# Full-tile V and P·V passes, remainders in either order, and a layer lag of eight in a two-layer segment-recurrent transformer kernel

## The chip, the cores and the metric

One NeuronCore of a Trainium2 chip runs the whole program. The metric is the device time of that core in microseconds (us). The kernel before takes 2775.58 us (median of 4 runs, 2775.19 to 2778.07). A ratio in this text is the mean time of one kernel's fast runs over the mean of the other's fast runs of the same rounds, so it is not quite the ratio of the medians that are quoted beside it. TensorE's matrix unit is called PE, VectorE DVE, ScalarE ACT.

## The reference

Two layers, each an attention block A with a recurrent memory and a feed-forward block B. The sequence of 2048 positions is cut into 64 segments of 32; eight memory columns come out of each segment and go into the next.

```python
for s in range(n_seg):                       # 64 segments, strictly one after the other
    h = concatenate([mem, x[segment s]])     # 8 + 32 = 40 rows of width 576
    q, k, v = h@Wq, h@Wk, h@Wv               # 32 heads of 128
    p = softmax(mask(q k^T * scale))
    o = (p v) @ Wo
    mem = o[:8]; out = o[8:]
# B: out = (silu(x@w1) * (x@w3)) @ w2        # 576 -> 4608 -> 576
x = x + A(layernorm(x)); x = x + B(layernorm(x))   # twice, with the same weights
```

## The kernel before

Layer 1 runs `LAG` segments behind layer 0, so most steps work on two segments at once (80 columns: 2 x 40). The work is cut into nodes, and a string of letters fixes PE's order: Q/q the Q/K projection and its 64-row remainder (576 = 4 x 128 + 64), S scores, T transposes of P, X/x and V/v the V projections of new x and of memory, P for P times V, O/o the output projection, F/f/W the feed-forward block. An opening string is followed by a block of four steps, repeated 11 times, and an end string. PE's results go to a memory called PSUM; there are seven banks of it (`bank` in the lines below) for everything but the output sum (`YB`).

```python
LAG = 7
...
def v_mm(self, t, b, strips, tail):          # V in strips of 32 columns, four side by side
    for c in ((4,) if tail else range(4)):
        for r in (0, 1):
            for p0, c0, q in strips:
                out = self.bk(b[r])[p0:p0 + 32, :]
                if tail: ...                 # 64-row remainder, eight strips side by side
                else:
                    w0 = ...
                    self.mm(out, HTt[:, c, c0:c0 + 32], W[:, c, w0:w0 + 512], c == 0, False, tile_position=(0, p0))
...
def pv(self, t, g, pts, vx, vm, b):          # 64-row halves: V of x and V of memory
    for hl in range(4):
        for m, s in todo:
            for ab in (0, 1):
                rr = slice(ab * R64, (ab + 1) * R64)
                self.mm(self.bk(b[ab])[...], self.T.V[rr, s.i, g % 2, ...], PT[rr, m, hl, :],
                        m == todo[0][0], m == 1, tile_position=(ab * R64, 0))
...
def load_v(self):                            # 512 rows in four loads of 128, the remainder in two of 64 partitions
    for c in range(4):
        self.dma(self.wv(False)[:, c, :], self.a.wv[c * P:(c + 1) * P, :])
    t = self.a.wv[4 * P:D, :].rearrange("p (k r n) -> p k r n", k=2, r=2)
    for r in (0, 1):
        self.dma(self.wv(True)[r * R64:(r + 1) * R64, :].rearrange("p (k n) -> p k n", k=2), t[:, :, r, :])
```

## Time and profile before

| | before |
|---|---|
| time, median | 2775.58 us |
| span of the profiled run | 2772.4 us |
| PE busy, PE idle | 2723.5 us, 48.9 us |
| DVE, ACT busy | 2047.1 us, 1091.0 us |
| PE idle in the first 100 us | 31.5 us |
| matmuls, changes of tile shape | 60919, 2138 |
| one block of four steps | 162.2 us |

Names in the profile lines, here and in the prediction: HT is the transposed input of attention; W, WV and WO are weights (W holds those of Q and K, and in turn those of the feed-forward block); QKT is Q and K, PB and PTS the probabilities before and after their transposes, XTB the transposed input of the feed-forward block. `64*128 64x80` is the part of PE's array in use (rows * columns), then the operand that streams through it (partitions x columns).

### The profile page before, as it was taken

The numbers are of one execution on the slowest core, as the hardware profiler recorded it, in microseconds if no ns is written. First come the engines' busy times: TensorE is split into PE (matmuls) and PEld (weight loads), VectorE is DVE, ScalarE is ACT, GpSimd is POOL, SyncE is SP. The second block draws the span as 40 slices with busy tenths as digits, with TensorE's granted clock in tenths as the row PEclk, the third lists the DMA queues.
The fourth block names the chain that finished last, engine by engine and source line by source line (L and its number), as shares of the span: only waits on it lengthen the run. The fifth ranks groups of instructions, "written<-read, shape, count | busy, mean of one in ns | idle before, by whom it ended". The sixth has DMA issues, their size and how long they took to land.

```text
span 2772.4 us, 136269 instructions
## 1 busy us (share of the span) xinstructions
PE 2723.5 (98%) x60919; PEld 2252.7 (81%) x60919; DVE 2047.1 (74%) x5584; ACT 1091.0 (39%) x3339; POOL 328.4 (12%) x399
## 2 busy tenths in 40 slices
PE   5999999999999999999999999999999999999999
PEld 4887888888888888888888888888888888878887
DVE  4677777777777777777777777777777777687776
ACT  1434343433434343343434334343433434343332
POOL 1111010110101011010101101010101101010110
PEclk9999999999999999999999999999999999999999
DMA  8062614244242424424152342415234241523467
GB/s 308 13 198 69 184 53 138 81 121 124 78 131 62 140 82 116 128 78 131 56 146 82 112 133 77 131 49 153 82 106 138 73 130 57 142 79 107 141 182 235
DMA packets 481691, 322.02 MB, mean 116 GB/s; under 512 B 26216, under 2 KB 476656, under 8 KB 479440
## 3 DMA queue, kind: packets, MB, share of 16 engines
q1 hardware_dynamic: 478080, 306.38, 37.7%
q8 instruction: 476, 7.80, 1.2%
q0 software_dynamic: 3024, 6.93, 0.9%
q14 instruction: 111, 0.91, 0.1%
HBM read 308.49 MB, written 2.36 MB: 112 GB/s over the span
## 4 chain that ended last, share of the span: by engine, by line
PE 96%; DMA 2%; ACT 1%; DVE 1%; issue 0%; SPq 0%; ACTq 0%; DVEq 0%
PE bank L547 82%; PE YB L547 14%; DMA W<-in_A_Wk_dram 1%; DMA W<-in_B_w_dram 1%; DMA WV<-in_B_w_dram 0%; SPq L556 0%; DMA W<-in_A_Wq_dram 0%; ACT OT L550 0%; DVE STAT L553 0%; ACT HT L550 0%; DVE SME L553 0%; ACT PTS L550 0%; DVE PB L553 0%; DVE PTS L553 0%; ACT QKT L550 0%
## 5 line engine op out<-in xcount | busy, mean ns | idle before, releaser
L547 PEld LDWEIGHTS <-W 128*128 128x128 bf16 (+1 forms) x29080 | 1231.6, 98 | 144.4 <-issue 37.7
L547 PE MATMUL bank<-HT,W 128*128 128x80 bf16 (+3 forms) x22720 | 816.4, 198 | 23.1 <-DMA W<-in_A_Wk_dram 12.1
L547 PE MATMUL bank<-XTB,W 128*128 128x256 bf16 (+1 forms) x6360 | 658.2, 261 | 1.6 <-ACT XTB L550 0.8
L906 POOL MEMSET PB<- 128x1024 bf16 x284 | 270.0, 951 | 2065.9 <-PE bank L547 1626.9
L550 ACT ACTIVATE QKT<-bank 128x64 bf16<-128x64 f32 (+1 forms) x1348 | 312.6, 315 | 445.0 <-PE bank L547 434.4
L547 PE MATMUL YB<-OT,WO 128*128 128x80 bf16 (+3 forms) x11360 | 429.2, 199 | 5.0 <-ACT OT L550 3.9
L547 PEld LDWEIGHTS <-WO 128*128 128x128 bf16 (+1 forms) x11360 | 385.2, 102 | 36.0 <-issue 17.4
L547 PE MATMUL bank<-WV,HT 128*32 128x512 bf16 (+1 forms) x6840 | 380.8, 382 | 0.0
L553 DVE CAST QKT<-bank 128x64 bf16<-128x64 f32 (+1 forms) x716 | 193.6, 316 | 243.5 <-PE bank L547 242.3
L547 PE MATMUL bank<-W2C,HTT 128*128 128x288 bf16 x2240 | 312.5, 287 | 0.2 <-issue 0.2
L553 DVE TENSOR_REDUCE STAT<-SME 104x8 f32<-104x320 f32 (+1 forms) x568 | 271.5, 478 | 44.8 <-ACT SME L550 41.2
L553 DVE TENSOR_TENSOR PB<-SME,STAT 40x128 bf16<-40x128 f32 (+1 forms) x1004 | 283.7, 321 | 12.9 <-DVE STAT L553 0.5
L547 PEld LDWEIGHTS <-HT 128*32 128x32 bf16 (+1 forms) x6840 | 150.2, 95 | 173.4 <-issue 48.1
L547 PEld LDWEIGHTS <-HTT 128*128 128x128 bf16 x2304 | 211.5, 98 | 57.4 <-issue 4.9
L553 DVE SCALAR_TENSOR_TENSOR XR<-bank,XR 128x288 f32<-128x288 f32 x576 | 241.2, 447 | 10.6 <-PE bank L547 4.6
L550 ACT ACTIVATE HTT<-bank 128x512 bf16<-128x512 f32 (+1 forms) x324 | 175.0, 549 | 182.8 <-PE bank L547 182.6
L550 ACT ACTIVATE SME<-SME 104x320 f32<-104x320 f32 (+1 forms) x284 | 133.4, 470 | 262.0 <-DVE SME L553 261.6
L553 DVE SCALAR_TENSOR_TENSOR HTT<-HTT,bank 128x512 bf16<-128x512 bf16 (+1 forms) x324 | 201.5, 622 | 41.2 <-ACT HTT L550 39.1
L550 ACT ACTIVATE PTS<-bank 128x320 bf16<-128x320 f32 (+1 forms) x386 | 146.5, 411 | 206.1 <-PE bank L547 143.0
L550 ACT ACTIVATE OT<-bank 128x320 bf16<-128x320 f32 (+1 forms) x358 | 141.1, 413 | 212.4 <-PE bank L547 212.0
L553 DVE TENSOR_TENSOR HTT<-HTT,bank 128x512 bf16<-128x512 bf16 (+1 forms) x324 | 203.6, 628 | 24.2
L550 ACT ACTIVATE V<-bank 128x512 bf16<-128x512 f32 x269 | 147.2, 596 | 173.9 <-PE bank L547 173.4
(64 smaller groups left out, 1676.3 us busy)
## 6 DMA issues: line engine op xcount, KB each, us to landing
W<-in_B_w_dram SPq DMA_DIRECT2D x612, 256.0 KB, 3.8
W2C<-in_B_w_dram SPq DMA_DIRECT2D x306, 288.0 KB, 3.2
W<-in_B_w_dram SPq DMA_DIRECT2D x612, 32.0 KB, 3.3
W<-in_B_w_dram SPq DMA_DIRECT2D x10, 512.0 KB, 8.2
WO<-in_A_Wo_dram SPq DMA_DIRECT2D x4, 1152.0 KB, 17.2
XR<-in_A_x_dram POOLq DMA_DIRECT2D x16, 288.0 KB, 3.1
W<-in_A_Wq_dram SPq DMA_DIRECT2D x4, 1024.0 KB, 8.4
W<-in_A_Wk_dram SPq DMA_DIRECT2D x4, 1024.0 KB, 15.0
```

The costliest lines, as they stand in the source:

```text
L547: self.ch("PE", self.nc.tensor.matmul(out, lhsT=lhsT, rhs=rhs, start=start, stop=stop, skip_group_check=True, **k))
L550: self.ch("ACT", self.nc.scalar.activation(*a, **k))
L553: self.ch("DVE", getattr(self.nc.vector, fn_)(*a, **k))
L906: return lambda n: self.ch("POOL", self.nc.gpsimd.memset(self.T.PB[:, pb.i], 0.0))
```

## The change

The intent is to spend less of PE on narrow tiles and on changing between tile shapes. V of the next segment's x and of this segment's memory share one full 128-column pass; P times V has one 128-row matmul per head instead of two 64-row halves; a main part and its remainder may run in either order, so that remainders can stand together; layer 1 runs eight steps behind. The weight loads change too: Q and K come in halves of the heads, and each 64-row remainder is folded onto 128 partitions in one transfer. In the new strings G and g are the full V pass and its remainder, p the transposes of the attention output, and w a second kind of W node.

```diff
-LAG = 7
+LAG = 8
...
+    def vg(self, t, g, b, tail):
+            for c in ((4,) if tail else range(4)):
+                for r in (0, 1):
+                    if tail: ...
+                    else:
+                        self.mm(self.bk(b[r])[:], HTt[:, c, 32:160], W[:, c, w0:w0 + 512], first and c == 0, c == 3)
...
-            for hl in range(4):
-                for m, s in todo:
-                    for ab in (0, 1):
-                        ... 64-row halves ...
+            for j in range(GH):
+                self.mm(self.bk(b[j // 4])[:, ...], self.T.V[:, self.head(g, j) // 4, ...],
+                        self.T.PTS[:, pts.i, j * nq:(j + 1) * nq], True, True)
...
+            for kind, wd in ((0, self.a.wq), (1, self.a.wk)):
+                self.dma(self.T.W[:, 8, kind * 2048:(kind + 1) * 2048], wd[4 * P:D, :].rearrange("p (r n) -> r p n", r=2))
...
+        return lambda n: self.dma(self.wv(True), self.a.wv[4 * P:D, :].rearrange("p (r n) -> r p n", r=2))
... (new order strings, slot bookkeeping, evictions of V by rows, W_O in eight loads, first loads of x and memory from ACT's queue)
```

## The prediction

> **What bounds the kernel now.** I read the page first: busy shares, then the chain that ended last, then PE's waits, then PE's timeline in a quiet stretch, because everything above says that only PE's own time counts.
>
> ```profile
> span 2772.4 us, 136269 instructions
> PE 2723.5 (98%) x60919; PEld 2252.7 (81%) x60919; DVE 2047.1 (74%) x5584; ACT 1091.0 (39%) x3339; POOL 328.4 (12%) x399
> PE 96%; DMA 2%; ACT 1%; DVE 1%; issue 0%; SPq 0%; ACTq 0%; DVEq 0%
> ```
>
> The reader is to see that PE is idle for 2772.4 - 2723.5 = 48.9 us in all, and that 96% of the chain is PE following PE. Where the idle time lies comes from the busy time by stretch (stretch, its length, then busy us of PE, PEld, DVE, ACT, POOL):
>
> ```profile
> 0.00:100.00 100.00, 68.47 (x1903) 53.56 (x1903) 50.91 (x142) 28.49 (x93) 17.86 (x34) 0.93 0.62 215
> 1000.00:1500.00 500.00, 499.23 (x10828) 415.20 (x10825) 374.82 (x1023) 201.87 (x611) 58.27 (x70) 1.00 0.36 105
> 1500.00:2000.00 500.00, 499.23 (x10844) 413.35 (x10838) 377.70 (x1029) 206.13 (x625) 57.51 (x68) 1.00 0.36 102
> ```
>
> The opening 100 us hold 31.5 us of the idle time, most of it the weights' arrival; in the middle it is 0.8 us in 500. So in the middle the time is the sum of what PE executes, and to price the change I need what each kind of matmul takes from its start to the start of the next. The mean duration of a row (about 200 ns) is latency and useless for this. The timeline of PE (start, length, instruction, count) gives it:
>
> ```profile
> 1418.13 4.19 PE L547 MATMUL bank<-WV,HT 128*32 128x512 bf16 x80
> 1422.25 0.43 PE L547 MATMUL bank<-QKT 128*64 128x40 bf16 x16
> ...
> 1429.79 1.15 PE L547 MATMUL bank<-W2C,HTT 128*128 128x288 bf16 x8
> 1430.77 1.31 PE L547 MATMUL bank<-HT,W 128*128 128x80 bf16 x32
> 1431.92 1.91 PE L547 MATMUL bank<-XTB,W 128*128 128x256 bf16 x16
> 1433.76 0.46 PE L547 MATMUL bank<-PTS,V 64*128 64x80 bf16 x16
> 1434.06 0.38 PE L547 MATMUL bank<-XTB,W 64*128 64x256 bf16 x4
> 1434.28 0.31 PE L547 MATMUL bank<-HT,W 64*128 64x80 bf16 x8
> 1434.52 2.47 PE L547 MATMUL YB<-OT,WO 128*128 128x80 bf16 x64
> 1436.82 0.45 PE L547 MATMUL bank<-sel,PB 104*128 104x80 bf16 x8
> 1437.20 0.34 PE L547 MATMUL YB<-OT,WO 128*64 128x80 bf16 x8
> ```
>
> Read it by differences of starts. Full tile, 80 columns: (1431.92 - 1430.77)/32 = 36 ns; the 64 of W_O: 2.30/64 = 36 ns. Full tile, 288 columns: 0.98/8 = 123 ns. P times V today is 16 matmuls of 64 rows, two side by side: 0.30 us, so 36 ns for a pair. The Q/K remainder is 4 pairs, 0.144 us, but 0.24 us pass before the next full-tile matmul: 0.096 us more. The transposes of P are 8 x 36 = 0.288 us, but 0.38 us pass before the next column-tiled one: 0.092 us more. Those two surpluses stand exactly where the tile shape changes. V: 80 rows are 16 passes of four strips and 2 of eight; 18 x 0.216 = 3.89 us (0.216 is the spacing of 512-column passes over the whole trace), and 4.12 us pass with two changes of shape: 0.23 for two. Over all 2138 changes the median surplus is close to 0.0975 us, whichever two shapes meet; I use that.
>
> Check of the rule on the kernel before: its 60919 matmuls priced so give 2507 us, its 2138 shape changes (counted in the built instruction list) 208 us, idle time 49 us; sum 2764 against a span of 2772.4. The 8 us left are 0.3%, partly the opening's granted clock of 0.93 in the stretch above.
>
> **What the Trainium skill says.** "TensorEngine Tiling (Array Packing)", Key Properties: changing the tiling mode drains the engine. It gives no figure; this trace gives 0.092 to 0.115 us. "TensorE: Matmul & The Clock Gate", "Wait — 56ns, not 53.3ns?": a warm matmul is spaced by N / 2.4 GHz plus about 2.5 ns, never under about 25 ns. For 80 columns that is 35.8 ns and for 512 it is 216 ns; the trace agrees (36 and 216). For 40 columns the floor holds: the trace's median is 25 ns, so a step with one layer costs more than half of a step with two. The same page, Part 3, "The mechanism": tiles in different row or column groups run concurrently, some 4 ns apart; the 16 in 0.30 us agree. "Perfetto Trace Analysis", "Optimization Strategy": a gap that repeats on the saturated engine can mean too few PSUM buffers. The kernel before has no such gap; the change could make one.
>
> **The change, part by part.** Counts before and after are from the two built programs.
>
> P times V in full tiles: 3712 half-row matmuls of 80 columns (1856 pairs at 36 ns) become 1792 full ones at 36 ns, and the 40-column ones likewise. A pair costs what a full one costs, so work alone does not fall (77.2 to 77.4 us). What falls is the shape: P times V no longer leaves the full shape.
>
> V in one pass: for two steps with both layers the old way was 5 nodes of 9 passes of 512 columns in strips; the new is 4 full-tile nodes and one in strips, again 45 passes. Again no work saved in the middle; at the ramps some passes go, and all V passes together fall from 332.4 to 319.1 us: -13.3.
>
> Layer 1 eight steps behind instead of seven: 56 steps of both layers and 16 of one, instead of 58 and 13. Q/K matmuls of 80 columns fall by 512 and of 40 rise by 768, and so on: Q/K projections +2.1, W_O +1.3, transposes, P times V and scores about -0.1. With the +0.2 of P times V already inside, +3.3.
>
> Remainders in either order and the new order: these let 64-row nodes stand next to each other. In the block of four steps, repeated 11 times, the changes of shape fall from 114 to 73: -41 x 0.0975 = -4.0 us of a block that lasts 162.2 us today (the same run of matmuls recurs at 1036.19, 1198.40 and 1360.61 us in the chain). In the whole program they fall from 2138 to 1430: -708 x 0.0975 = -69.0 us. All of it lies on PE, and PE is the path.
>
> Sum of PE: -13.3 + 3.3 - 69.0 = -79 us.
>
> Beside PE: V is copied out of PSUM in 342 instructions now (269 ACT, 73 DVE) and in 864 then, since each bank holds rows for different places. One of 512 columns takes 596 ns on ACT and 689 on DVE, however many partitions. At the new split (560 and 304) V adds 173 us to ACT and 159 to DVE. Q/K copies move the other way, from DVE to ACT. With the durations of the rows before I estimate DVE 2047 to about 2105 us (78% of a shorter span) and ACT 1091 to about 1355 (50%). Neither becomes the bound on average.
>
> The loads are split by head halves, so first Q/K work can start earlier, but V and W_O arrive as late as before (the first V matmul stood at 43.55 us). I give -2 us. For new waits I add 5 us. Span 2772.4 - 79 - 2 + 5 = 2696; measured times are 3.5 us over the span (2775.85 against 2772.4): 2700 us, 2.7% less.
>
> **The rivals.** First, PSUM: a full-tile V node holds two of seven banks from its first matmul until half is copied, P times V of that group has run, and the other half is copied. A wait of 0.1 us in each of 288 groups would be 29 us and the result 2724: within 2%. For it speaks that seven banks serve everything and DVE is busier; against it, that PE waits 0.8 us per 500 today with nodes held just as long between main part and remainder. Second, the drains might hide copies PE would otherwise wait for; then removing them turns them into waits, and only some 20 us come off: 2755. For it: nearly every change of shape is a new node. Against: the same surplus at any two shapes, and almost no waits beside it. Third, V and P times V themselves get faster in full tiles, by fewer weight loads; then 2670. Against: spacing already equals the streaming of columns. Fourth, the extra one-layer steps starve at the ends: the recurrence has less to hide behind; 5 to 10 us.
>
> **Range and chances.** Work and shape changes are counted, their prices measured to perhaps 8%: +-6 us. The skew is upward, from waits. Range 2672 to 2732. The 2% line is 2720.3, so 20 us of unforeseen waits are needed to miss it: faster 0.82, same 0.17, slower 0.01.
>
> **What would show it.** Right: PE still 98% busy, a block of four steps near 158 us, P times V as 8 matmuls in about 0.29 us with no surplus, full V passes of 0.216 us, PE idle about 50 us in all. Wrong: PE waiting for V or bank copies by ACT or DVE over and over in the middle (first rival), surplus still 0.1 us at each new node without a change of shape (second), or idle time in the first 100 us well over 31 us (fourth).

## More of the kernel before

The prediction shows how the middle is read. Here is what it passed over quickly, the opening. First, who PE waited for (us in total, times, longest), then the queue that issues the loads (start, time taken, what, how many):

```profile
PE bank L547 <- DMA W<-in_A_Wk_dram: 12.1, 5, 3.0
```

```profile
6.92 0.55 SPq L556 DMA_DIRECT2D W<-in_A_Wq_dram  x1
9.40 0.47 SPq L556 DMA_DIRECT2D W<-in_A_Wk_dram  x1
11.88 13.71 SPq L556 DMA_DIRECT2D WV<-in_A_Wv_dram  x6
27.40 19.65 SPq L556 DMA_DIRECT2D WO<-in_A_Wo_dram  x4
```

The reader is to see that the weights set the pace of the first 30 us, in an orderly row: the two lone transfers of W are the 64-row remainders, V follows at 11.88 us, and W_O at 27.40.

## The result, and the profile after

The changed kernel takes 2748.91 us (median of 4 runs, 2746.57 to 2753.3; ratio 0.9904, 95% interval 0.989 to 0.9918). It is correct and 1% faster, where 2.7% was forecast, and the time lies above the stated range. Against the 2% line it counts as the same, to which the prediction gave 0.17. The profiled run is the slowest of the four. Its head and its chain by engine:

```profile
span 2751.5 us, 126617 instructions
PE 2657.0 (97%) x55783; PEld 2234.0 (81%) x55783; DVE 2137.9 (78%) x5480; ACT 1362.0 (49%) x3920; POOL 333.2 (12%) x400
PE 91%; DVE 3%; ACT 2%; DMA 2%; issue 1%; SPq 1%; POOL 0%; DVEq 0%; ACTq 0%
```

PE's busy time fell by 66.5 us, but PE now idles 2751.5 - 2657.0 = 94.5 us, 45.6 more than before. The busy time by stretch (same columns as in the prediction) says where:

```profile
0.00:100.00 100.00, 40.48 (x1038) 31.51 (x1039) 37.56 (x98) 21.27 (x59) 11.29 (x24) 0.86 0.65 214
1000.00:1500.00 500.00, 497.12 (x9889) 417.82 (x9886) 400.01 (x1015) 251.46 (x730) 57.13 (x68) 1.00 0.37 106
```

The first 100 us hold 59.5 us of idle time instead of 31.5. The middle holds 2.9 in 500 instead of 0.8. Both traces keep every matmul of their programs (60919 and 55783), so the boundaries between opening, blocks and end are found by counting, and each stretch can be compared with its price: matmuls at the durations of the prediction, plus 0.0975 us for each change of shape.

| stretch (us) | before | priced for after | after | PE idle, before to after |
|---|---|---|---|---|
| opening | 549.9 | 549.9 - 11.4 - 160 x 0.0975 = 522.9 | 558.7 | 37.0 to 67.7 |
| 11 blocks | 1784.5 | 1784.5 - 451 x 0.0975 = 1740.5 | 1750.4 | 2.8 to 10.6 |
| end | 434.1 | 434.1 + 1.4 - 97 x 0.0975 = 426.0 | 438.1 | 5.2 to 12.0 |

Of the excess over the price, 35.8 + 9.9 + 12.1 = 57.8 us, the opening has 62%, and the growth of idle time explains 45.3 (30.7 of it in the opening). The other 12.5 us stand in no wait that the profile lists; a lower granted clock (0.86 against 0.93 in the first 100 us) or an error of the prices would do, and neither was tested. So the opening is the first thing to ask about. Whom PE waited for, over the whole run:

```profile
PE bank L580 <- DMA W<-in_A_Wk_dram: 19.2, 7, 12.8
PE bank L580 <- DMA WV<-in_A_Wv_dram: 13.0, 3, 9.4
...
PE bank L580 <- DVE HT L586: 8.8, 11, 0.8
PE bank L580 <- DMA W<-in_A_Wq_dram: 8.4, 1, 8.4
```

Three single waits, 12.8, 9.4 and 8.4 us, are 30.6 us. PE's timeline shows what stands behind them:

```profile
26.24 0.21 PE L580 MATMUL bank<-HT,W 64*128 64x40 bf16 x2 [8.36 <-DMA W<-in_A_Wq_dram]
39.30 0.96 PE L580 MATMUL bank<-HT,W 64*128 64x40 bf16 x30 [12.84 <-DMA W<-in_A_Wk_dram]
...
70.91 3.99 PE L580 MATMUL bank<-WV,HT 64*32 64x512 bf16 x48 [9.39 <-DMA WV<-in_A_Wv_dram]
```

All three are matmuls of 64 rows: the remainders of Q, K and V, which are the three loads that were folded into one transfer each. The queue that issues them, and the share of the 16 DMA engines in use (next to last column) in stretches before and during such a load:

```profile
6.82 0.63 SPq L589 DMA_DIRECT2D W<-in_A_Wq_dram  x1
7.55 4.66 SPq L589 DMA_DIRECT2D W<-in_A_Wk_dram  x1
12.26 18.67 SPq L589 DMA_DIRECT2D W<-in_A_Wq_dram  x4
```

```profile
8.00:12.00 4.00, 0.94 (x10) 0.66 (x10) 2.23 (x10) 0.96 (x1) 0.56 (x1) 1.00 1.03 380
16.00:20.00 4.00, 1.88 (x57) 1.76 (x53) 0.00 (x0) 0.00 (x0) 0.00 (x0) 1.00 0.13 53
```

Between 16 and 20 us the DMA engines move 53 GB/s at a share of 0.13, which is 0.13 x 16 = 2.1 engines' worth, and only packets of 4096 bytes pass. Each took 159 ns, so a load of 128 such packets on two engines takes 64 x 0.159 = 10.2 us. V's remainder agrees: PE's last V matmuls before it could start at 60.47 us, those of the remainder at 70.91, 10.4 us later. The four loads behind took 18.67 us to issue, where comparable ones in the first microseconds took 2.66.

The middle agrees with the prices. Full V and P times V in a block:

```profile
857.25 2.22 PE L580 MATMUL bank<-WV,HT 128*128 128x512 bf16 x10
859.31 1.56 PE L580 MATMUL bank<-HT,W 64*128 64x80 bf16 x40
...
872.90 0.45 PE L580 MATMUL bank<-PTS,V 128*128 128x80 bf16 x8
873.19 3.15 PE L580 MATMUL YB<-OT,WO 128*128 128x80 bf16 x96
```

Eight full V passes and a pair of remainders take 2.06 us: 9 x 0.216 + 0.0975 = 2.04. Eight P times V take 0.29 us, with no surplus before W_O. A block lasts 159.2 us (the same run of matmuls recurs at 1354.82, 1513.98 and 1673.19 us), priced at 158.2. Over the ten blocks from 717 to 2309 us, the list of PE's waits has one entry:

```profile
PE bank L580 <- DVE HT L586: 8.0, 10, 0.8
```

It is 0.8 us at each block's start. The new block opens with two 64-row remainders, which need the memory columns as DVE has summed them; the timeline there shows PE going on at 1513.79, when the first of DVE's two additions is done (it ends at 1513.73; the line gives the two together):

```profile
1513.30 0.23 ACT L583 ACTIVATE YO<-YB 64x80 f32<-64x80 f32 x1
1513.57 0.36 DVE L586 TENSOR_TENSOR HT<-YB,YO 64x16 bf16<-64x16 f32 x2 [2.02 <-ACT YO L583]
1513.79 1.90 PE L580 MATMUL bank<-HT,W 64*128 64x80 bf16 x48 [0.80 <-DVE HT L586]
```

### The profile page after: what moved, and what is told of

Its sections match the earlier page's. It is cut to its first block, busy times and chain, and to the rows that moved or that the text cites.

```text
span 2751.5 us, 126617 instructions
## 1 busy us (share of the span) xinstructions
PE 2657.0 (97%) x55783; PEld 2234.0 (81%) x55783; DVE 2137.9 (78%) x5480; ACT 1362.0 (49%) x3920; POOL 333.2 (12%) x400
## 4 chain that ended last, share of the span: by engine, by line
PE 91%; DVE 3%; ACT 2%; DMA 2%; issue 1%; SPq 1%; POOL 0%; DVEq 0%; ACTq 0%
PE bank L580 79%; PE YB L580 13%; ACT V L583 1%; DMA WV<-in_A_Wv_dram 1%; SPq L589 1%; DVE V L586 1%; DVE STAT L586 1%; DVE SME L586 1%; DMA W<-in_A_Wk_dram 1%; DVE XR L586 0%; ACT SME L583 0%; DMA W<-in_A_Wq_dram 0%; DVE PB L586 0%; DMA W<-in_B_w_dram 0%; ACT HT L583 0%
## 5 line engine op out<-in xcount | busy, mean ns | idle before, releaser
L580 PE MATMUL bank<-XTB,W 128*128 128x256 bf16 (+3 forms) x6360 | 652.3, 262 | 2.2 <-ACT XTB L583 1.4
L583 ACT ACTIVATE QKT<-bank 128x256 bf16<-128x256 f32 (+2 forms) x1533 | 373.5, 307 | 361.7 <-PE bank L580 339.3
L580 PE MATMUL YB<-OT,WO 128*128 128x80 bf16 (+3 forms) x11520 | 409.6, 198 | 5.0 <-issue 4.6
L583 ACT ACTIVATE V<-bank 32x512 bf16<-32x512 f32 (+1 forms) x560 | 318.4, 585 | 144.6 <-PE bank L580 139.3
L580 PE MATMUL bank<-WV,HT 128*32 128x512 bf16 (+4 forms) x3240 | 369.8, 385 | 13.0 <-DMA WV<-in_A_Wv_dram 13.0
L586 DVE TENSOR_TENSOR PB<-SME,STAT 40x128 bf16<-40x128 f32 (+4 forms) x912 | 275.7, 336 | 15.0 <-DVE STAT L586 0.5
L580 PEld LDWEIGHTS <-HT 128*32 128x32 bf16 (+4 forms) x3240 | 138.4, 96 | 160.9 <-issue 39.9
L583 ACT ACTIVATE OT<-bank 128x320 bf16<-128x320 f32 (+1 forms) x403 | 150.5, 404 | 183.1 <-PE bank L580 180.6
L586 DVE CAST V<-bank 64x512 bf16<-64x512 f32 (+1 forms) x304 | 208.1, 685 | 34.0 <-PE bank L580 27.9
L586 DVE CAST QKT<-bank 128x128 bf16<-128x128 f32 (+4 forms) x515 | 141.5, 316 | 105.3 <-PE bank L580 102.4
```

The lines of the kernel that those rows point to most:

```text
L580: self.ch("PE", self.nc.tensor.matmul(out, lhsT=lhsT, rhs=rhs, start=start, stop=stop, skip_group_check=True, **k))
L583: self.ch("ACT", self.nc.scalar.activation(*a, **k))
L586: self.ch("DVE", getattr(self.nc.vector, fn_)(*a, **k))
```

## The experiments

The theory, T: a folded remainder load runs on two DMA engines and holds up what is issued after it. Rivals: R, the half-row loads with their small packets and greater number are slow; S, one-layer steps starve for the recurrence, whatever the loads do. The base for runs 1 to 3 is the changed kernel. All eight runs gave correct results.

**Run 1, remainder loads cut in two.**

```diff
-                self.dma(self.T.W[:, 8, kind * 2048:(kind + 1) * 2048], wd[4 * P:D, :].rearrange("p (r n) -> r p n", r=2))
+                for r in (0, 1):
+                    self.dma(self.T.W[r * R64:(r + 1) * R64, 8, kind * 2048:(kind + 1) * 2048], wd[4 * P:D, r * 2048:(r + 1) * 2048])
(the same for the remainder of V)
```

> The changed kernel with each of its three merged remainder loads (Q, K and V, 64 rows folded to 2 x 64 partitions in one transfer) cut into two transfers of 64 rows. Theory T (the merged form runs on 2 of 16 DMA engines, about 10 us for 0.5 MB, and holds up the loads behind it): PE's waits of 8.4, 12.8 and 9.4 us in the opening go, PE idle in the first 100 us falls from 59.5 to about 30 us, time about 2720 us. Rival R (the half-row loads with 2 KB packets and their larger number are what is slow): about 2747. Rival S (one-layer steps starve for the recurrence, whatever the loads do): about 2745.

Measured: 2725.62 us (2725.3 to 2727.07), ratio 0.9825 (0.981 to 0.9839), 23.3 us less than the changed kernel. Busy time by stretch, the first 100 us and the same four microseconds as above, in which most of the remainders' packets of 4096 bytes now pass together with others:

```profile
0.00:100.00 100.00, 65.78 (x1743) 51.69 (x1744) 57.33 (x152) 37.63 (x105) 15.67 (x29) 0.90 0.65 215
```

```profile
16.00:20.00 4.00, 2.27 (x60) 2.11 (x60) 0.00 (x0) 0.00 (x0) 0.00 (x0) 1.00 1.04 229
```

The engines are at 1.04 instead of 0.13, and idle PE time in the first 100 us falls from 59.5 to 34.2 us, near the 31.5 of before. The longest waits for K, V and Q weights are now 2.3, 3.8 and 0.2 us, where they were 12.8, 9.4 and 8.4. T holds; the time is 5.6 us above what it expected.

**Run 2, whole rows, folded remainders kept.**

```diff
-                    w, d = (v.rearrange("p (r h n) -> p r h n", r=2, h=2)[:, :, half] for v in (...))
-                    self.dma(w, d)
+                    self.dma(self.T.W[:, 4 * kind + c, :], wd[c * P:(c + 1) * P, :])
```

> The changed kernel with the Q and K weights again loaded in whole rows (8 KB packets, 8 transfers instead of 16), the merged remainder loads kept. Theory T: the remainders still take about 10 us each on 2 engines, time 2740 to 2755. Rival R: the opening is as before the change, about 2720. Rival S: about 2749.

Measured: 2747.57 us (2745.71 to 2748.53), ratio 0.99. Larger packets and half as many transfers alone change nothing, and the long waits stand as they were (14.2, 9.5 and 9.3 us for K, V and Q): R falls.

**Run 3, both edits.**

> Both edits: whole rows and cut remainders. Theory T: about the time of the first run, within 6 us of it, the half-row order being worth a few us only: 2720 to 2728. Rival R: as with whole rows alone. Rival S: about 2749.

Measured: 2722.01 us (2717.45 to 2723.06), ratio 0.9807. That is 3.6 us less than run 1, so loading by head halves, which was meant to start Q/K work earlier, does not pay; the two ratios' intervals overlap a little, so its size is rough. As the cause of the long waits S falls too: the same steps with the same recurrence lost their long waits when the loads changed.

**Run 4, the cost put into the kernel before.** The V remainder of the kernel before is folded into one transfer, nothing else.

```diff
-            for r in (0, 1):
-                self.dma(self.wv(True)[r * R64:(r + 1) * R64, :].rearrange("p (k n) -> p k n", k=2), t[:, :, r, :])
+            self.dma(self.wv(True).rearrange("p (k n) -> p k n", k=2), t.rearrange("p k r n -> r p k n"))
```

> The kernel BEFORE with its V remainder loaded in the merged form (2 x 64 partitions in one transfer) and nothing else changed. Theory T: this load takes about 10 us instead of about 2.5 and V comes that much later, time 2781 to 2787 (5 to 11 us more than before). Rivals R and S: 2776, as before.

Measured: 2778.88 us against 2775.64 for before, ratio 1.0016 (1.0001 to 1.0031). The wait is there, as PE's list of waits in this run says:

```profile
PE bank L547 <- DMA WV<-in_A_Wv_dram: 7.4, 1, 7.4
```

The sign is as T said, though the interval only just excludes no change; the size is not: +3.2 us instead of 5 to 11. The four W_O loads behind the folded one took longer to issue, as T says, 28.83 us against the 19.65 shown for before:

```profile
25.38 28.83 SPq L556 DMA_DIRECT2D WO<-in_A_Wo_dram  x4
```

PE's idle time in the first 100 us grew by only 4.0 us (35.5 against 31.5), so part of the 7.4 us stands where PE had waited for something else: the idle 2.1 us just before V's first matmuls in the kernel before are 0.4 here.

For runs 5 to 8 run 3 was the base, made again on the same chip.

**Run 5, run 3 again.**

> The kernel of cut remainders and whole rows again, as the base for the three others of this call. All theories: 2722 within 4 us, as before.

Measured: 2720.29 us (2716.33 to 2722.89), ratio 0.9801.

**Run 6, the first letters of the block turned.**

```diff
-    "qqQpQqqpQQnv...
+    "QqqpQqqpQQnv...
```

> The same with the first four letters of the repeated block turned from q q Q p to Q q q p, so that the main part of the Q/K projection, which needs only the ACT part of the memory columns, stands first and the 64-row remainder, which needs the DVE sum too, comes 1.15 us later. Theory U (the 0.8 us that PE waits for DVE at each of the 11 block starts is this order's alone): that wait goes and one change of shape per block comes, (0.8 - 0.1) x 11 = 7.7 us less, about 2714. Rival V (DVE at 78% and 7 PSUM banks are short, and the wait only moves elsewhere in the block): 2720 to 2724.

Measured: 2713.64 us (2712.1 to 2717.33), ratio 0.9782 (0.9768 to 0.9795): 6.6 us less than run 5 and faster than both given kernels. The wait for DVE at the block starts is gone; a smaller one for ACT's part of the same columns came in its place, 8.2 us in all against 4.4 in run 5:

```profile
PE bank L579 <- ACT HT L582: 8.2, 19, 1.6
```

A block lasts 158.6 us (848.30 to 1006.92 in the chain). U holds, with most of its size (7.7 us were expected).

**Run 7, changes of shape alone.** Run 6 with twelve letters of the block moved, one of the four places:

```diff
-...SFPOTOwPWTOPFOoooow...      (the remainders o together)
+...SFPOoTOowPWTOoPFOow...      (three of four apart)
```

> The kernel of the run before this with the same matmuls, but three of the four W_O remainders of each step set apart from one another among full-tile work: 264 more changes of tile shape and nothing else. Theory P (a change costs PE 0.0975 us wherever it stands, since almost no wait lies beside it): 25.7 us more, about 2740. Rival D (the drain overlaps with copies PE would have waited for anyway): 0 to 8 us more.

Measured: 2742.22 us (2741.38 to 2742.84), 28.6 us more than run 6: 28.6 / 264 = 0.108 us for each change. P holds, D falls.

**Run 8, the full V pass cut into column halves.**

```diff
-                        self.mm(self.bk(b[r])[:], HTt[:, c, 32:160], W[:, c, w0:w0 + 512], first and c == 0, c == 3)
+                        for h in (0, R64):
+                            self.mm(self.bk(b[r])[h:h + R64, :], HTt[:, c, 32 + h:96 + h], W[:, c, w0:w0 + 512], first and c == 0, c == 3,
+                                    tile_position=(0, h))
```

> The same base with each full-tile V pass cut into two column halves side by side (64 columns each, same output, twice the instructions and weight loads), remainders likewise: 214 more changes of shape. Theory P: a pair streams as one, so only the changes count, 214 x 0.0975 = 20.9 us more, about 2735. Rival F (the full tile is itself faster, by fewer weight loads): 35 us more or above, 10 us or more beyond the changes of shape.

Measured: 2735.33 us (2731.59 to 2735.53), 21.7 us more than run 6: 0.101 us for each of the 214 changes, and 0.8 us left over for the narrower tiles themselves, less than the spread of the runs. F falls.

## Why the prediction was wrong

**The step that failed** is the sentence on the loads: "The loads are split by head halves, so first Q/K work can start earlier, but V and W_O arrive as late as before ... I give -2 us." It looked at the order of the loads and not at their form. V did not arrive as late as before, but later: its first matmul stood at 55.22 us instead of 43.55, and its remainder could start only at 70.91. In place of -2 us, the folded remainders cost about 23 us (changed kernel against run 1), and loading by halves of the heads about 4 more (run 1 against run 3). The Trainium skill had the rule. "DMA: Bandwidth & Descriptors", "Why a DMA increments its semaphore by 16 and not by 1", says that the largest number of engines up to 16 is taken that divides the slowest dimension of both patterns that is not of size one, and its "Rules for kernel authors" warn of an outermost dimension under 16. The folded pattern has the 2 outermost. The trace agrees: a share of 0.13, or 2.1 of the 16 engines, and a share of 1.04 once the 64 rows are outermost. The prediction looked up the matmuls and not the loads that the diff adds.

**What bounds the kernel, and the prices:** right. The surplus at a change of shape was put at 0.0975 us; runs 7 and 8, which add such changes and nothing else, measure 0.108 and 0.101. That P times V and V save nothing by themselves is what the trace (0.29 us for eight, 0.216 us a pass) and run 8 show.

**The block:** 158.2 us were predicted and 159.2 measured. The difference is the wait of 0.8 us for DVE at each start; with the letters turned it is 158.6. The 5 us given for new waits were thus too few: the blocks alone gained 7.8 us of idle time, and the end 6.8.

**DVE and ACT:** DVE was estimated at 2105 us and took 2137.9; ACT 1355 and took 1362.0. Neither became the bound, as said.

**The rivals:** the first, PSUM banks held by V, does not show: in the ten blocks PE waits neither for a copy of V nor for a bank. The second, drains that hide waits, fell in run 7, the third in run 8. For the fourth, starving at the ends, the prediction named "idle time in the first 100 us well over 31 us" as the sign. The sign came, with another cause: after run 1 only 34.2 us are left. A sign that two causes share does not tell them apart. At the other end the rival is neither shown nor excluded: the end string of run 6 still takes 435.6 us against 426.0 priced, which is within the 5 to 10 us that the rival gave, and no run took those steps away.

**What stays open:** run 6 is still 13.6 us above the 2700 predicted. Its profiled run (2717.33 us, the slowest of its four) lies 8.2 us over the price in the opening, 3.2 in the blocks (with their 11 changes more) and 9.6 in the end. In the profiled run of the changed kernel the end string holds 5.3 us of waits that the profile puts down to nothing ("issue"), against 0.7 before. The runs of one kernel spread over up to 7 us, and no experiment separated the waits of the end, nor the small ones left in the opening. Taking the eighth step of lag away alone was not tried: the order strings are built for it. The traces of runs 1 to 3 and 5 to 7 lack 84 matmul records each (55699 of 55783), so their idle totals are a little too high and only stretches and single waits are read from them.

## What to carry to other kernels

When one engine is full, price its work from start to start, count the changes of mode in the built program, and the middle of a kernel can be forecast to under 1%. Then give the same care to the part that the full engine does not rule, here the first 70 us: look at the outermost dimension of every load that a diff adds or reshapes. Where an order begins with the piece whose input comes last, turning two letters can be worth more than its extra change of mode.

## What the Trainium skill lacked or had wrong

- "TensorEngine Tiling (Array Packing)", Key Properties, says that a change of mode drains the engine but not what it costs. Here it is close to 0.0975 us as the median surplus of 2138 changes, and 0.101 and 0.108 us in runs 8 and 7.
- "TensorE: Matmul & The Clock Gate", "Back-to-back issue gap", gives for streams of weight load and matmul about 81 ns at 128 columns and 131 ns at 512. Here such streams run at 56 ns (16 matmuls from 2719.43 to 2720.33 us of the changed kernel) and at 216 ns (the median between full V matmuls of the changed kernel), which is what the same page's simple formula says.
- "DMA: Bandwidth & Descriptors" has the rule for the number of engines; these runs add a size for its effect behind the slow transfer: the next four loads took 18.67 us to issue, against 2.66 us for four at the start.
